# Windowed attention into a gated mixture: mixture scores, tails and values as fp32 products in quarters of the array, in a new order

## The chip, the core and the metric

One core of one Trainium2 chip runs the whole program. The metric is the device time of one execution in microseconds (us), the median of several runs.

## What is computed

Windowed causal attention over 8 batches, 8 heads and 576 positions, and then a mixture of four small attention experts over its output, of which a gate keeps two for each position. Cut to what matters:

```python
scores = scale * np.matmul(q, k.transpose(0, 1, 3, 2))          # head_dim 64
scores = np.where(mask, scores + bias[None], -1000000000.0)     # 0 <= rel < 128
attn = softmax(scores)
x = (attn @ v).transpose(0, 2, 1, 3).reshape(B, S, H * D)       # 8 x 576 x 512
for e in range(4):                                              # experts, 64 wide
    q, k, v = x @ wq[e], x @ wk[e], x @ wv[e]
    a = softmax(np.where(causal, -1000000000.0, scale * (q @ k.transpose(0, 2, 1))))
    out += gate_weight[:, :, e] * (a @ v @ wo[e])               # two experts of four
```

## The kernel before

The 576 positions are four blocks of 128 (`NQ = 4`) and a tail of 64 (`TAIL`). The attention takes one pair of heads at a time, 32 pairs `g`, four to a batch `b`. The mixture takes one pair of experts at a time, `pr` = 0 and 1 for each batch, with row `j` = 0 or 1 of the pair in the lower or upper 64 partitions. So a (b, pr) unit occurs 16 times.

The tensor engine (PE) is used whole (128*128) or cut into tiles: 128*64 are two column halves, 64*128 two row halves, and 64*64 four quarters. Tiles that share no rows and columns work side by side. An fp32 product takes two passes, so it shows as two matmul rows of the trace; a float32r product or a transpose shows as one.

Attention works in quarters, in fp32 (`attn_s`, `attn_pv`), and its values already come from two PSUM tiles, one for each half of the keys, which are added on VectorE. The mixture works otherwise:

- `qkproj` writes q and k of an expert pair as a float32r cast (`QH`, `KH`) and a float32r remainder (`QL`, `KL`), each by one cast and one subtraction from PSUM.
- `moe_s` makes the scores of the four blocks as three float32r terms (two for block 0), 22 matmuls on row halves of 64*128 for each (b, pr), over the full causal width 128(i+1) of a block of 128 query rows.
- `moe_s_tail` makes the tail's scores for both rows j at once from a block-diagonal copy of the tail queries (`QJ`, rounded into place by `pool_round`), with six matmuls of 288 columns on the whole array for each (b, pr).
- `moe_t` transposes the probabilities (`turn` does so in pairs of 64*128 tiles; the last tail block is one 128*128 transpose).
- `moe_pv` multiplies them by the values, 8 fp32 matmuls on column halves (128*64) into one PSUM tile, then a cast to `AH` and a subtraction from PSUM to `AL`; `moe_pv_tail` does the same for the tail, 10 matmuls.
- `moe_wo` multiplies `AH` and `AL` by the split output weights `WOH` and `WOL`: for each block of 128 positions first the three terms of pr 0 (WOH·AH, WOL·AH, WOH·AL), then the three of pr 1.

At the start the program works on block 0 and 1 of the four head pairs of batch 0 (`half_s` with x = 0) as soon as their first loads are there, while PE repeats a filler matmul (`warm`).

What sets the order: all engine operations are recorded, and `plan` replays them by the numbers of a packed table `ORDER`, which also chooses the engine where an operation has two (`nc.any`) and says where filler matmuls stand. `place` issues them, so that nearly every instruction has line 1189 in the trace (1225 in the kernel after). Each engine and each DMA queue runs its own instructions in that order. The loads go through SyncE's queue (SP), four of the start through ScalarE's.

## Time and profile before

| | us |
|---|---|
| median of 3 runs | 472.25 |
| lowest and highest run | 471.92, 472.99 |
| the profiled execution | 473.2 |
| its span, first to last instruction | 471.4 |
| busy in it: PE, VectorE (DVE), ScalarE (ACT), GpSimd (POOL) | 462.7, 409.3, 370.5, 222.7 |

The profiled execution is 0.95 us above the median, and 1.8 us of it lie outside the span. A timeline row tells when a run of like matmuls starts and how long it lasts. Ends of matmuls are modelled: the next row starts before the end of the last one, so what a run costs is read from its start to the next row's start.

### The profile page before, as it was taken

The numbers are of one execution on the slowest core, as the hardware profiler recorded it, in microseconds if no ns is written. First come the engines' busy times: TensorE is split into PE (matmuls) and PEld (weight loads), VectorE is DVE, ScalarE is ACT, GpSimd is POOL, SyncE is SP. The second block draws the span as 40 slices with busy tenths as digits, with TensorE's granted clock in tenths as the row PEclk, the third lists the DMA queues.
The fourth block names the chain that finished last, engine by engine and source line by source line (L and its number), as shares of the span: only waits on it lengthen the run. The fifth ranks groups of instructions, "written<-read, shape, count | busy, mean of one in ns | idle before, by whom it ended". The sixth has DMA issues, their size and how long they took to land.

```text
span 471.4 us, 17542 instructions
## 1 busy us (share of the span) xinstructions
PE 462.7 (98%) x6380; PEld 403.8 (86%) x6380; DVE 409.3 (87%) x1894; ACT 370.5 (79%) x1409; POOL 222.7 (47%) x464
## 2 busy tenths in 40 slices
PE   7999999999999999999999999999999999999996
PEld 5788999897889789797898987898789897899775
DVE  6999999979998998879989798798999979966852
ACT  5968879989978688796989798897976959833952
POOL 4833968183916346261470907426263623561430
PEclk9999999999999999999999999999999999999999
DMA  7899410345320653150441281602731030300033
GB/s 202 266 221 246 112 52 1 77 103 141 108 80 0 139 142 117 29 140 1 115 129 37 80 189 39 180 2 61 205 121 38 3 86 2 120 1 1 3 113 112
DMA packets 29862, 44.99 MB, mean 95 GB/s; under 512 B 9424, under 2 KB 15824, under 8 KB 29776
## 3 DMA queue, kind: packets, MB, share of 16 engines
q1 hardware_dynamic: 29040, 43.42, 34.0%
q8 instruction: 50, 0.82, 0.8%
q10 hardware_dynamic: 736, 0.46, 0.4%
q14 instruction: 36, 0.29, 0.2%
HBM read 34.42 MB, written 9.44 MB: 93 GB/s over the span
## 4 chain that ended last, share of the span: by engine, by line
PE 84%; DMA 5%; SPq 3%; DVE 3%; ACT 2%; POOL 1%; issue 1%; DVEq 0%
PE ps L1189 84%; DMA w<-in_hd 4%; SPq L1189 3%; DVE w L1189 2%; ACT w L1189 2%; POOL w L1189 1%; DMA w<-in_wall 1%; DVE ps L1189 1%; DVE WL L1189 0%; DVE ALm L1189 0%; ACT AHm L1189 0%; DVE mr L1189 0%; DVE nm L1189 0%; POOL QJm L1189 0%; DVE ALTm L1189 0%
## 5 line engine op out<-in xcount | busy, mean ns | idle before, releaser
L1189 ACT COPY w<-ps 128x256 f32<-128x256 f32 (+2 forms) x232 | 92.4, 443 | 29.8 <-PE ps L1189 21.3
L1189 PE MATMUL ps<-wx,WH 128*128 128x288 f32 (+2 forms) x512 | 110.4, 300 | 0.0
L1189 ACT ACTIVATE w<-w,nm 128x128 f32<-128x128 f32 x252 | 98.9, 397 | 7.3 <-DVE nm L1189 5.8
L1189 POOL TENSOR_SCALAR w<-w,mr,w 128x256 f32<-128x256 f32 (+3 forms) x128 | 78.2, 622 | 43.2 <-DVE mr L1189 24.1
L1189 POOL TENSOR_SCALAR w<-w,r 128x128 f32<-128x128 f32 x177 | 64.6, 378 | 68.3 <-PE ps L1189 25.4
L1189 PEld LDWEIGHTS ps<-wx,WH 128*128 128x128 f32 x512 | 83.2, 190 | 1.5 <-issue 0.3
L1189 ACT ACTIVATE w<-w,mnm 128x512 f32<-128x512 f32 (+3 forms) x128 | 71.2, 558 | 10.0 <-DVE mnm L1189 9.4
L1189 DVE TENSOR_TENSOR w<-ps,tmt 128x768 f32<-128x768 f32 (+3 forms) x96 | 72.5, 770 | 3.3 <-PE ps L1189 2.2
L1189 DVE CUSTOM_DVE_ANT_0 w<-ps,tbt 128x128 f32<-128x128 f32 x288 | 71.7, 283 | 1.1
L1189 PE MATMUL ps<-wx,WL 128*128 128x288 f32 (+2 forms) x256 | 71.9, 298 | 0.0
L1189 PE MATMUL ps<-WH,wx 128*128 128x260 f32 x288 | 61.5, 285 | 0.0
L1189 PE MATMUL ps<-w 64*64 64x192 f32 (+3 forms) x1256 | 58.6, 304 | 2.3 <-DMA w<-in_hd 1.7
L1189 PE MATMUL ps<-idt,w 64*128 64x64 f32 (+1 forms) x1152 | 58.6, 230 | 1.0 <-POOL w L1189 0.9
L1189 PEld LDWEIGHTS ps<-idt,w 64*128 64x128 f32 (+1 forms) x1152 | 47.4, 139 | 11.0 <-issue 3.4
L1189 PE MATMUL ps<-w,vt 64*64 64x192 f32 (+3 forms) x1344 | 56.3, 283 | 0.0
L1189 PEld LDWEIGHTS ps<-w,vt 64*64 64x64 f32 (+1 forms) x1344 | 50.0, 133 | 5.7 <-DVE r L1189 0.6
L1189 DVE COPY_PREDICATED ps<-mkt,ps 128x128 f32<-128x128 int32 (+2 forms) x160 | 49.2, 329 | 5.4 <-PE ps L1189 5.0
L1189 PEld LDWEIGHTS ps<-w 64*64 64x64 f32 (+1 forms) x1256 | 44.0, 134 | 8.6 <-DMA w<-in_hd 2.7
L1189 DVE CUSTOM_DVE_ANT_0 w<-ps,mtt 128x256 f32<-128x256 f32 (+2 forms) x96 | 49.8, 551 | 0.8 <-PE ps L1189 0.4
L1189 PEld LDWEIGHTS ps<-WH,wx 128*128 128x128 f32 x288 | 48.0, 189 | 0.8 <-issue 0.3
L1189 ACT ACTIVATION_READ_ACCUMULATOR w<-w,nm 128x1 f32 x252 | 48.6, 193 | 0.0
L1189 PE MATMUL ps<-w,w 128*64 128x64 f32 (+4 forms) x576 | 48.0, 319 | 0.0
(111 smaller groups left out, 947.5 us busy)
## 6 DMA issues: line engine op xcount, KB each, us to landing
w<-in_hd SPq DMA_DIRECT2D x56, 288.0 KB, 4.6
vt<-in_vd SPq DMA_DIRECT2D x28, 320.0 KB, 3.7
out<-w SPq DMA_DIRECT2D x31, 256.0 KB, 2.5
w<-in_hd SPq DMA_DIRECT2D x14, 128.0 KB, 3.5
w<-in_hd SPq DMA_DIRECT2D x56, 32.0 KB, 3.7
w<-in_wall SPq DMA_DIRECT2D x4, 386.0 KB, 6.6
out<-w SPq DMA_DIRECT2D x8, 128.0 KB, 3.3
vt<-in_vd SPq DMA_DIRECT2D x4, 192.0 KB, 3.8
```

The lines of the kernel that those rows point to most:

```text
L1189: getattr(getattr(tc.nc, e), m)(*a, **k)
```

## The change

Mixture scores, tails and values become fp32 products in 64*64 quarters. `qkproj` writes q and k once, unsplit, into `KK`; `QH`, `QL`, `KL` and `QJ` are gone. `moe_s` gives each half of 64 query rows its own causal width; in odd blocks the two row halves are swapped, with a second bias table `mts` for them. `moe_s_tail` treats both pairs of a batch at once, and `moe_t` transposes all five tail blocks in `turn`. `moe_pv` splits the keys between the row halves, into two PSUM tiles, which are then drained, added, rounded and subtracted.

```diff
-        hi, lo = (QH, QL) if isq else (KH, KL)
-        act_copy(hi[:, pr, sl], o, n)
-        dve_sub(lo[:, pr, sl], o, hi[:, pr, sl].bitcast(F32), n)
-        if isq and half == 1:
-            for x, q in ((0, QH), (1, QL)):
-                for j in range(2):
-                    d = slice(D * j, D * j + D)
-                    pool_round(QJ[d, pr, x, d], q[d, pr, S - TAIL :].bitcast(F32))
+        evac(KK[:, 0 if isq else 1, pr, sl], o)
...
         for i in blocks:
             n = P * (i + 1)
-            m = n if i else 2 * P
-            for x, (q, k) in enumerate(terms if i else terms[:2]):
-                for j in range(2):
-                    d = slice(D * j, D * j + D)
-                    k2 = k[d, pr, :n] if i else KK[d, :, pr, :P]
+            for j in range(2):
+                d = slice(D * j, D * j + D)
+                for y in range(2):
+                    m = P * i + D * (y ^ i & 1)
                     nc.tensor.matmul(
-                        ss[j][:, o : o + m], q[d, pr, P * i : P * (i + 1)], k2, start=(x == 0), stop=(x == (2 if i else 1))
+                        ss[j][D * y : D * y + D, o : o + m + D], KK[d, 0, pr, m : m + D], KK[d, 1, pr, : m + D], start=True, stop=True
                     )
...
-                softmax_block(ss[j][:, o : o + n], pt, mtt[:, 512 - n : 512] if i else pt, nm[:, c : c + 1], n)
+                softmax_block(ss[j][:, o : o + n], pt, (mts if i % 2 else mtt)[:, 512 - n : 512], nm[:, c : c + 1], n)
```

```diff
-    def moe_s_tail(b, pr):
+    def moe_s_tail(b):
         st = m2s[b]
-        nm, sm = st[pr, "nm"], st[pr, "sm"]
-        pt = MPL[pr]
         ss = []
+        stats(b, 1)
         for half in range(2):
-            s = ps_s.tile([P, 512], F32, tag="s", name=f"msl{b}_{pr}_{half}")
-            ss.append(s)
+            ss.append([ps_s.tile([P, 512], F32, tag="s", name=f"msl{b}_{half}_{j}") for j in range(2)])
             sl = slice(HALF * half, HALF * (half + 1))
-            for k, (x, w) in enumerate(((0, KH), (1, KH), (0, KL))):
-                nc.tensor.matmul(s[:, :HALF], QJ[:, pr, x, :], w[:, pr, sl], start=(k == 0), stop=(k == 2))
...
+            for j in range(2):
+                d = slice(D * j, D * j + D)
+                for pr in range(2):
+                    nc.tensor.matmul(
+                        ss[half][j][D * pr : D * pr + D, :HALF], KK[d, 0, pr, NQ * P :], KK[d, 1, pr, sl], start=True, stop=True
+                    )
...
+                softmax_block(ss[half][j][:, :HALF], MPL[j][:, sl], bias, dst, HALF, init=init)
+        for j in range(2):
```

```diff
-        parts = ([(0, 0), (1, 0)], [(0, 1), (0, 3), (1, 1), (1, 3)], [(0, 2), (1, 2)], [("tail", c) for c in range(NQ)])[u]
-        n = 8 if u < 2 else 4
-        pc = (tw if u < 2 else big2).tile([P, n * P], F32, tag="pt", name=f"mpt{b}_{pr}_{u}")
+        parts = ([(0, 0), (1, 0)], [(0, 3), (0, 1), (1, 1), (1, 3)], [(0, 2), (1, 2)], [("tail", c) for c in range(NQ + 1)])[u]
+        n = (8, 8, 4, 5)[u]
+        pc = (big2 if u == 2 else tw).tile([P, n * P], F32, tag="pt", name=f"mpt{b}_{pr}_{u}")
...
-            evac(pc.rearrange("p (a n) -> p a n", n=P)[:, :, D * h : D * h + D], ts[h][:, :n, :], n * D)
-        if u == 3:
-            t = ps_t.tile([P, P], F32, tag="t", name=f"mt{b}_{pr}_4")
-            nc.tensor.transpose(t, st["p"][pr, "tail"][:, NQ * P :], idt)
-            pc = st["pt"][pr, "tail", NQ] = tr.tile([P, P], F32, tag="pt", name=f"mpt{b}_{pr}_4")
-            evac(pc, t, P)
-
-    def moe_pv(b, pr, c):
+            if u == 3:
+                evac(v[:, :, D * h : D * h + D], ts[h][:, :n, :])
+            elif u == 1:
+                o = D - D * h
+                evac(spread(pc, o, (3 * P, 3), (P, 2)), spread(ts[h].rearrange("p a n -> p (a n)"), 0, (3 * D, 3), (D, 2)))
+                evac(v[:, 2:6:3, D - o : 2 * D - o], ts[h][:, 2:6:3, :])
+            else:
+                evac(spread(pc, D * h, (2 * P, n // 2), (3 * D - P * h, 2)), ts[h][:, :n, :].rearrange("p (a b) n -> p a b n", b=2))
```

```diff
+    def moe_pv(b, pr):
         st = m2s[b]
+        xa, ya = (ps_a.tile([P, 512], F32, tag="m", name=f"{n}{b}_{pr}") for n in ("ma", "mb"))
...
-        n = 512 - P * c
-        for j in range(2):
-            e = 2 * pr + j
-            nc.tensor.matmul(
-                acc[D * j : D * j + D, P * c :], V2[:, c, D * e : D * e + D], st["pt"][pr, j, c][:, :n],
-                start=(c == 0), stop=True, skip_group_check=True,
-            )
-        if c == NQ - 1:
-            act_copy(AH[:, pr, :512], acc, 512)
-            dve_sub(AL[:, pr, :512], acc, AH[:, pr, :512].bitcast(F32), 512)
-
-    def moe_pv_tail(b, pr):
+        for c in range(NQ):
+            for y, dst in enumerate((xa, ya)):
+                r, f = slice(D * y, D * y + D), D * y
+                for j in range(2):
+                    e = 2 * pr + j
+                    nc.tensor.matmul(
+                        dst[D * j : D * j + D, P * c + f :], V2[r, c, D * e : D * e + D], st["pt"][pr, j, c][r, f : 512 - P * c],
+                        start=(c == 0), stop=True, skip_group_check=True,
+                    )
+        tmp = big2.tile([P, DM], F32, tag="xs", name=f"ma{b}_{pr}t")
+        evac(tmp, xa)
+        nc.vector.tensor_tensor(tmp[:, D:], tmp[:, D:], ya[:, D:], add)
+        rnd(AH[:, pr, :512], tmp)
+        ssub(AL[:, pr, :512], tmp, AH[:, pr, :512].bitcast(F32))
```

```diff
+        ta, tb_ = (ps_t.tile([P, 512], F32, tag="t", name=f"mal{b}_{y}") for y in range(2))
         for c in range(NQ + 1):
-            for j in range(2):
-                e = 2 * pr + j
-                src = pt[pr, "tail", c][:, D * j : D * j + D]
-                nc.tensor.matmul(
-                    acc[D * j : D * j + D, :TAIL], V2[:, c, D * e : D * e + D], src,
-                    start=(c == 0), stop=(c == NQ),
-                )
+            for y, dst in ((0, ta), (1, tb_))[c // NQ :]:
+                r = slice(D * y, D * y + D)
+                for pr in range(2):
+                    for j in range(2):
+                        e = 2 * pr + j
+                        nc.tensor.matmul(
+                            dst[D * j : D * j + D, D * pr : D * pr + D], V2[r, c, D * e : D * e + D], pt[j, "tail", c][r, D * pr : D * pr + D],
+                            start=(c + pr == 0), stop=True, skip_group_check=True,
+                        )
         o = TAIL * (b % 2)
-        ht, lt = AHT[:, pr, o : o + TAIL], ALT[:, pr, o : o + TAIL]
-        act_copy(ht, acc[:, :TAIL], TAIL)
-        dve_sub(lt, acc[:, :TAIL], ht.bitcast(F32), TAIL)
+        ht, lt = AHT[:, :, o : o + TAIL], ALT[:, :, o : o + TAIL]
+        tt = p2.tile([P, P], F32, tag="xq2", name=f"xm{b}", bufs=1)
+        evac(tt, ta[:, :P])
+        nc.vector.tensor_tensor(tt, tt, tb_[:, :P], add)
+        v = tt.rearrange("p (a n) -> p a n", n=TAIL)
+        rnd(ht, v)
+        ssub(lt, v, ht.bitcast(F32))
```

In the attention the four tail-score matmuls of a head pair all read the upper 64 partitions, where the tail keys get a tile `ku` of their own. Before, two read the lower (64 columns each) and two the upper (128 columns each); now the upper ones make all 64 and 128 columns.

```diff
+        nc.sync.dma_start(ku[D:], a[D:, QW + NQ * P : QW + S])
         nc.sync.dma_start(r[D:, 2 * S + TAIL :], a[D:, QW + (NQ - 1) * P : QW + NQ * P])
         nc.sync.dma_start(r[D:, 2 * S : 2 * S + TAIL], a[D:, NQ * P : S])
-        prepped[g] = (None, None, None, vt, r)
+        prepped[g] = (None, None, ku, vt, r)
 
...
-            lo, up = e[:D], e[D:]
+            up, s = e[D:], ss[1]
             x, m = 2 * S, S + (NQ - 1) * P
-            c, w = slice(3 * P, 3 * P + TAIL), slice(3 * P, 4 * P)
-            nc.tensor.matmul(ss[0][:D, c], lo[:, NQ * P : S], lo[:, m + P :][:, :TAIL], start=True, stop=True)
-            nc.tensor.matmul(ss[0][D:, c], lo[:, x : x + TAIL], lo[:, x + TAIL : x + 2 * TAIL], start=True, stop=True)
-            nc.tensor.matmul(ss[1][:D, w], up[:, x : x + TAIL], up[:, x + TAIL :], start=True, stop=True)
-            nc.tensor.matmul(ss[1][D:, w], up[:, :TAIL], up[:, m : m + P], start=True, stop=True)
-            nc.vector.copy_predicated(ss[1][:, c], mkt[:, P:], ss[0][:, c])
+            q0, q1, k0, k1 = up[:, x : x + TAIL], up[:, :TAIL], up[:, x + TAIL :], up[:, m : m + 3 * D]
+            nc.tensor.matmul(s[:D, 2 * P + D : 3 * P], q0, ku[D:], start=True, stop=True)
+            nc.tensor.matmul(s[D:, P : P + D], q1, k1[:, P:], start=True, stop=True)
+            nc.tensor.matmul(s[:D, 3 * P :], q0, k0, start=True, stop=True)
+            nc.tensor.matmul(s[D:, 3 * P :], q1, k1[:, :P], start=True, stop=True)
+            nc.vector.copy_predicated(s[:D, 3 * P : 3 * P + TAIL], mkt[:D, P:], s[:D, 2 * P + D : 3 * P])
+            nc.vector.copy_predicated(s[D:, 3 * P : 3 * P + TAIL], mkt[D:, P:], s[D:, P : P + D])
```

At the start the first blocks are computed causally, block 1 over all its 256 keys, with a bias table `FT` (kept in `KK`) that holds the mask, and without the predicated copies. The transposes of these blocks go from 16 to 24. The DMAs of `tmt` and `mkt` move from ScalarE's queue to SP's, the zeroing of PSUM goes, and `ORDER` is a new table.

```diff
-        part = products(ss, 2 * x, [q, q], k, tbt[:, p], 2, 5 * x)
+        if x == 0:
+            first_blocks(g, ss, q, k, FT[:, NP_ - 1 - g])
+            return
...
+    def first_blocks(g, ss, q, k, tb):
+        nm, sm, pt = state[g, 0]
+        for i in range(2):
+            n = P + P * i
+            for h in range(2):
+                d = slice(D * h, D * h + D)
+                for y in range(2):
+                    m = P * i + D * y
+                    nc.tensor.matmul(
+                        ss[h][D * y : D * y + D, P * i : P * i + n], q[h][d, m : m + D], k[d, :n], start=True, stop=True
+                    )
...
+                v = pt[:, 3 * h + i : 3 * h + 2 * i + 1, :]
+                bias = tb[:, h, 1 - i :, :].bitcast(F32)
+                softmax_block(a, v, bias, nm[:, c : c + 1], P + P * i)
+                exp_block(None, v, nm[:, c : c + 1], sm[:, c, 0:1], P + P * i)
...
-    fetch(0, 1, 0)
+    for g in range(4):
+        fetch(g, 1, 0)
     nc.scalar.dma_start(idt, ident)
-    nc.scalar.dma_start(tmt, tm)
-    nc.scalar.dma_start(mkt[:, P:], mk[:, P:])
-    nc.vector.tensor_scalar(mkt[:, :P], tbt[:, 3, 0, :], -1.0e6, None, op0=ALU.is_lt)
+    nc.vector.tensor_scalar(FT[:, 3, :, 0, :], tbt[:, 3, 0:3:2], -1.0e6, NEG, op0=ALU.is_ge, op1=mul)
+    nc.vector.tensor_tensor(FT[:, 3, :, 0, :], FT[:, 3, :, 0, :].bitcast(F32), tbt[:, 3, 1:4:2], add)
+    nc.gpsimd.tensor_scalar(FT[:, 3, :, 1, :], tbt[:, 3, 0:3:2], 1.0, 0.0, op0=mul, op1=add)
...
-    for t in ps_s.real:
-        tc.nc.vector.memset(t[D:, : 3 * P].rearrange("p (a n) -> p a n", n=P)[:, :, :D], 0.0)
```

Weights are split in two column pieces (`wprep`), and there are more buffers for probabilities: pools of 8, 4, 3 and 6 slots (`pp`, `tw`, `tr`, `big2`) become 9, 6, none and 5.

SP's queue at the start of the program, before. `w_90` and `w_91` get the heads of the first blocks (`in_hd`), `w_83` and `w_86` the weights, `vt` the values:

```order
L1189 DMA w_90<-in_hd 64x2x256 x4
L1189 DMA w_91<-in_hd 64x2x256 x4
L1189 DMA w_90<-in_hd 128x2x128
L1189 DMA w_90<-in_rd 128x2x320
L1189 DMA w_90<-in_hd 64x2x256 x2
L1189 DMA w_83<-in_wall 128x772
L1189 DMA vt_128<-in_vd 128x256
```

And after, where `w_91` and `w_92` are these two:

```order
L1225 DMA ku_148<-in_hd 64x64
L1225 DMA ku_151<-in_hd 64x64
L1225 DMA ku_156<-in_hd 64x64
L1225 DMA mts<-in_mt 64x512 x2
L1225 DMA w_91<-in_hd 64x2x256 x4
L1225 DMA w_92<-in_hd 64x2x256 x4
L1225 DMA w_91<-in_rd 128x2x320
L1225 DMA w_91<-in_hd 64x2x256 x2
L1225 DMA vt_125<-in_vd 128x256
L1225 DMA vt_126<-in_vd 128x256
L1225 DMA w_83<-in_wall 128x772
```

Five DMAs that the program needs later now stand ahead of the first heads' loads, and the values stand ahead of the first weights.

PE in the middle of the program, batch 2, from the values of pr 1 on. Before (`KKm,QHm` and `KKm,QLm` are scores, `WOH,AHm` is the output product that needs these values):

```order
L1189 MATMUL ps_74<-w_95,w_86 64x512 x2
L1189 MATMUL ps_74<-w_96,w_86 64x384 x2
L1189 MATMUL ps_74<-w_102,w_86 64x256 x2
L1189 MATMUL ps_74<-w_96,w_86 64x128 x2
L1189 MATMUL ps_72<-KKm,QHm 128x512
L1189 MATMUL ps_69<-KKm,QHm 128x512
L1189 MATMUL ps_72<-KKm,QLm 128x512
L1189 MATMUL ps_69<-KKm,QLm 128x512
```

And after:

```order
L1225 MATMUL ps_70<-KKm 64x512
L1225 MATMUL ps_70<-KKm 64x448
L1225 MATMUL ps_74<-w_95,w_87 64x512 x2
L1225 MATMUL ps_72<-w_95,w_87 64x448 x2
L1225 MATMUL ps_74<-w_99,w_87 64x384 x2
L1225 MATMUL ps_72<-w_99,w_87 64x320 x2
L1225 MATMUL ps_69<-KKm 64x64
L1225 MATMUL ps_69<-KKm 64x128
L1225 MATMUL ps_76<-KKm 64x64
L1225 MATMUL ps_76<-KKm 64x128
```

Scores and values now share the quarters and stand between one another, where there was a change of tile shape between them; the values fill two PSUM tiles. Between the last values matmul and the first output product stand 30 matmuls in the order before (the 22 scores, a transpose and 7 projections of 288 columns), and 39 in the order after (26 transposes of 64*128 tiles, one on the whole array and 12 projections).

## Rows read from the trace of the kernel before

**Rows 1.** The page: busy time by engine, and the chain that ended last.

```profile
PE 462.7 (98%) x6380; PEld 403.8 (86%) x6380; DVE 409.3 (87%) x1894; ACT 370.5 (79%) x1409; POOL 222.7 (47%) x464
PE 84%; DMA 5%; SPq 3%; DVE 3%; ACT 2%; POOL 1%; issue 1%; DVEq 0%
```

**Rows 2.** Busy time by window: from:to, length, busy us of each engine (x instructions).

```profile
200.00:300.00 100.00, 99.33 (x1406) 88.62 (x1399) 86.63 (x411) 85.69 (x331) 49.71 (x105) 1.00 0.36 95
300.00:400.00 100.00, 99.37 (x1405) 86.55 (x1405) 91.75 (x423) 81.26 (x315) 39.84 (x88) 1.00 0.26 74
```

**Rows 3.** PE's timeline in batch 2: start, length, operation (modelled end).

```profile
213.41 2.18 PE L1189 MATMUL ps<-idt,w 64*128 64x64 f32 x64
215.53 2.37 PE L1189 MATMUL ps<-w,w 128*64 128x512 f32 x16
217.83 0.50 PE L1189 MATMUL ps<-KKm,QHm 64*128 64x512 f32 x2
...
219.85 0.33 PE L1189 MATMUL ps<-idt,w 128*128 128x128 f32 x1
...
220.41 0.43 PE L1189 MATMUL ps<-wx,WH 128*128 128x288 f32 x2
220.68 0.29 PE L1189 MATMUL ps<-wx,WL 128*128 128x288 f32 x1
...
220.94 0.39 PE L1189 MATMUL ps<-WOH,AHm 128*128 128x512 f32 x1
```

**Rows 4.** PE's timeline: one set of attention scores in quarters, and the row behind.

```profile
50.93 1.42 PE L1189 MATMUL ps<-w 64*64 64x192 f32 x32
52.29 0.39 PE L1189 MATMUL ps<-WH,wx 128*128 128x260 f32 x1
```

**Rows 5.** PE's timeline: tail scores of the mixture between output products.

```profile
397.11 0.40 PE L1189 MATMUL ps<-WOH,ALm 128*128 128x512 f32 x1
397.34 0.57 PE L1189 MATMUL ps<-KKm,QJm 128*128 128x288 f32 x3
397.75 0.40 PE L1189 MATMUL ps<-WOH,AHm 128*128 128x512 f32 x1
```

**Rows 6.** PE's timeline: tail values of the mixture.

```profile
464.44 0.57 PE L1189 MATMUL ps<-w,w 128*64 128x64 f32 x12
464.94 0.39 PE L1189 MATMUL ps<-WOH,AHm 128*128 128x256 f32 x1
```

**Rows 7.** PE's timeline where attention scores end and attention values begin.

```profile
224.85 0.32 PE L1189 MATMUL ps<-w,vt 64*64 64x192 f32 x1
224.86 0.27 PE L1189 MATMUL ps<-w 64*64 64x128 f32 x1
```

**Rows 8.** SP's queue at the start: when DMAs are issued, and how long that takes.

```profile
0.73 5.97 SPq L1189 DMA_DIRECT2D w<-in_hd  x9
...
9.18 0.90 SPq L1189 DMA_DIRECT2D vt<-in_vd  x2
```

**Rows 9.** PE's timeline at the start: the first scores, and later ones.

```profile
4.81 3.69 PE L1189 MATMUL ps<-w 64*64 64x128 f32 x52
...
12.77 1.53 PE L1189 MATMUL ps<-w 64*64 64x192 f32 x32
```

**Rows 10.** Groups by shape: operation xcount | busy us, mean ns | idle before, releasers.

```profile
L1189 ACT COPY w<-ps 128x512 f32<-128x512 f32 x99 | 56.1, 590 | 16.2 <-PE ps L1189 15.4
...
L1189 POOL TENSOR_TENSOR wx<-w,wx 128x512 fp32r<-128x512 f32 x17 | 22.2, 1309 | 0.5
...
L1189 DVE TENSOR_TENSOR w<-w,ps 128x448 f32<-128x448 f32 x28 | 17.1, 612 | 1.2 <-ACT w L1189 0.6 <-PE ps L1189 0.2 <-issue 0.2
...
L1189 DVE TENSOR_TENSOR KKm<-ps,KKm 128x288 fp32r<-128x288 f32 x28 | 12.5, 450 | 2.6 <-ACT KKm L1189 2.3
...
L1189 POOL TENSOR_SCALAR wx<-w 128x512 fp32r<-128x512 f32 x19 | 11.8, 624 | 27.5 <-DVE w L1189 23.1 <-ACT w L1189 3.7 <-DVE ps L1189 0.3
...
L1189 DVE TENSOR_TENSOR ALm<-ps,AHm 128x512 fp32r<-128x512 f32 x16 | 11.0, 686 | 1.1 <-ACT AHm L1189 0.8
```

More of the change, by code (lines that the diff above doesn't have):

```diff
@@ L312, in attn_moe_kernel @@
     prepped = {}
+    half = {}
     SM = [cp.tile([P, 9, 2], F32, name=f"sm{k}") for k in range(2)]
@@ L663, in attn_moe_kernel, with terms @@
     AA = {}
+    def terms(late):
+        return sorted(((c, j) for c in range(4) for j in range(3)), key=lambda z: late and z[1] == 2)
     def vproj(b, t):
@@ new lines, in moe_s_tail @@
+            for j in range(2):
+                nm = st[j, "nm"]
+                bias = mtt[:, 0:HALF] if half == 0 else mtt[:, 512:]
+                init = BIG if half == 0 else nm[:, 9:10]
+                dst = nm[:, 9:10] if half == 0 else nm[:, 8:9]
+                softmax_block(ss[half][j][:, :HALF], MPL[j][:, sl], bias, dst, HALF, init=init)
+        for j in range(2):
+            nm, sm = st[j, "nm"], st[j, "sm"]
+            for half in range(2):
+                sl = slice(HALF * half, HALF * (half + 1))
+                exp_block(ss[half][j][:, :HALF], MPL[j][:, sl], nm[:, 8:9], sm[:, 16 + half : 17 + half], HALF)
+            st["p"][j, "tail"] = MPL[j]
@@ L943, in wload @@
             nc.sync.dma_start(mtt, mt)
+            for y in range(2):
+                nc.sync.dma_start(mts[D * y : D * y + D], mt[D - D * y : 2 * D - D * y, : NQ * P])
         wst[c] = w
@@ L1000, in f @@
             if tail:
-                moe_pv_tail(b, pr)
+                moe_pv_tail(b)
             else:
-                for c in range(NQ):
-                    moe_pv(b, pr, c)
+                moe_pv(b, pr)
             live[0] -= 0 if tail else 7
```

370 lines of the change are left out of this document (181 added, 189 removed).

## The prediction

> **What bounds the kernel now.** I read the page first: PE is busy for 462.7 of 471.4 us, VectorE for 409.3, and PE makes 84% of the chain that ended last [rows 1]. Then the windows: in the body PE works for 99.3 of each 100 us, while VectorE has 8 to 13 us to spare, ScalarE 14 to 19 and POOL half [rows 2]. So the body is worth what PE has to do, and an edit on another engine counts only if it delays PE or uses up that slack. Last the timelines, from the start of one run to the start of the next. Two places do not follow this rule: the start, where PE waits for loads and for the first softmax [rows 8, 9], and the end.
>
> **Prices on PE.** A run inside one tile shape loses less than one that ends with a change of shape: the modelled end lies 0.17 us behind the next start where the shape stays (397.11 + 0.40 against 397.34) [rows 5], but only 0.06 to 0.07 us where it changes (52.35 against 52.29; 217.90 against 217.83) [rows 3, 4]. A change costs 0.10 us. The set of attention scores takes 52.29 - 50.93 = 1.36 us; less one change, 1.26 us for 32 rows, four side by side, is 8 passes of 192 columns, 0.82 ns for a column and pass [rows 4]. The values give 0.86: 16 rows, two side by side, 2560 column passes in 2.30 - 0.10 = 2.20 us [rows 3]. I use 0.84.
>
> **Scores, 16 units.** Before, 217.83 to 219.85 is 2.02 us, or 1.92 without its change [rows 3]. After, each row half runs the widths 64, 128, ... 512, 2304 columns, over two quarters side by side, 1152 columns in each; two passes: 2304 x 0.84 ns = 1.94 us. Three cheap terms become one dear one at half the width: +0.02 x 16 = +0.3 us.
>
> **Tail scores.** Three matmuls of 288 take 0.41 us, 0.137 each [rows 5]; 12 to a batch are 1.64 us. After, four quarters of 2 x 288 columns and two passes: 0.97 us. -0.67 x 8 = -5.4 us. This is the largest term, since before half of the block-diagonal operand was zeros.
>
> **Values.** The column halves already fill the array, so quarters bring no more throughput: the lower row half has 1280 columns, 2.15 us against 2.20. The upper half has 1024, 1.72 us. If the halves keep step, the unit costs what the longer one does: 0 to -0.8 us in all, taken as 0.
>
> **Attention tails.** 64 columns more on the upper quarters, two passes, 0.108 us, 28 times (the first four pairs are made otherwise): +3.0 us if the halves keep step; the lower half gets 64 columns less, -3.0 us, if they do not.
>
> **Tail values.** Before, 12 rows take 0.50 us, less a change 0.40, 0.033 each [rows 6]; 40 rows to a batch are 1.33 us. After, 10 matmuls of 64 columns in the upper quarters, two passes: 1.08 us (8 in the lower: 0.86). -0.25 x 8 = -2.0 us.
>
> **Transposes and changes of shape.** 32 tail transposes more in 64*128 tiles at 2.12 / 64 = 0.033 us [rows 3] are +1.1 us; the 16 on the whole array that go gave back about as much, at 0.09 us each (219.85 is one, before the projections), -1.4 us. I set both to 0. Along PE the tile shape changes 153 times in the order before and 125 times after; 28 x 0.10 = -2.8 us.
>
> In step, PE's sum is 0.3 - 5.4 + 0 + 3.0 - 2.0 + 0 - 2.8 = **-6.9 us**.
>
> Do the halves keep step? Where scores end and values begin, a values matmul starts at 224.85, ahead of a scores matmul at 224.86 [rows 7]: a half runs ahead, but by one pass, not a unit. The Trainium skill has both answers: "TensorEngine Tiling (Array Packing)", section Key Properties, says that tiles operate independently; "TensorE: Matmul & The Clock Gate", Part 3, section The mechanism, says that matmuls start and end strictly in program order. By the second the sum is the -6.9 us; by the first it is that of the rival below. The row leans to the second.
>
> **The other engines.** VectorE and ScalarE lose the split of q and k: subtractions of 450 ns [rows 10], for keys and for queries, 64 in all, against 16 additions of 612 ns and some copies. POOL takes most of the new subtractions at 1309 ns; it is idle half the time [rows 2]. None becomes the bound. What is late next is the chain behind the values. Before: a cast and a subtraction of 0.69 us. After: drain 0.59, add 0.61, round 0.62, subtract 1.31 on POOL, 3.13 us [rows 10]. The cover in batch 2: before, 217.83 to 220.94, 3.1 us [rows 3]; after, 26 transposes (0.86), one more (0.09), 12 projections at 0.135 (1.62) and two or three changes, 2.8 us, and then the three products of pr 0 at 0.23 [rows 5], 0.7 us. The rounded part is wanted after 3.5 us and is there after 1.8, the remainder is wanted after 4.0 and there after 3.1. It holds, with some 0.9 us left for hand-overs and queueing; in the last batch less stands between. Bounds: 0, and 8 x 0.5 = 4; taken: **+0.8 us**.
>
> **The start.** SP needs 5.97 us for nine DMAs, 0.66 each, and 0.45 for a `vt` [rows 8]. Five DMAs now stand ahead of the first heads' loads: 5 x 0.45 to 5 x 0.66 = 2.3 to 3.3 us. Nothing hides that: the first scores start at 4.81 when their load has landed, and PE runs without long gaps only from 12.77 on [rows 9], so what the first loads lose goes through to the end. The weights and `vt` come later by as much. In return VectorE drops eight predicated copies there, but ScalarE has exponentials twice as wide and PE eight more transposes; I let these cancel. Bounds: 0 (the wait only replaces another one, as the masks come from ScalarE's queue) and 3.3; taken: **+2.8 us**. The eight PSUM memsets that go lay ahead of the first load's landing and are worth 0.
>
> **Sum.** 473.2 - 6.9 + 0.8 + 2.8 = 469.9 us for an execution like the profiled one, which stood 0.95 us above the median; against the median, **469.0 us**.
>
> **The rivals.**
> - The row halves run on their own, each through a whole run of quarters. Then the lower one sets the end: values -0.8, attention tails -3.0, tail values -0.47 x 8 = -3.8, with scores, tail scores and changes -15.5; the upper gives -7.7 + 3.0 - 2.0 and so -14.6. The slower counts, -14.6 in place of -6.9: 461.3 us; half way, 465. For it: scores and values now alternate in one shape. Against: the lead of one pass [rows 7].
> - Slower: the chain behind the values is late. Its four steps cross ScalarE, VectorE and POOL, of which the first two are busy for some 81 to 92% [rows 2], so each can queue for half a microsecond behind something else, and the 0.9 us are gone twice over. With 1 us of PE waiting behind the values of pr 1 in each of the eight batches: 469.0 + 8 = 477 us. It decides from 0.4 us a batch, where the gain of 3.25 is used up. For it: the cover shrinks from 3.1 us, of which 1.3 were needed, to one of 4.0, of which 3.1 are. Against: in the body PE waits for under 1 us in 100 now.
> - No gain: the changes of shape bring nothing, since the work between them drains anyway (+2.8), and the start costs 3.3 (+0.5): 472.3 us.
>
> **How the numbers follow.** Chances: the forecast 0.48, halves on their own (wholly or half) 0.14, slower 0.23, no gain 0.15. From this kernel's runs, 0.2% (0.95 us) is about what a measurement can tell from no change, so faster is below 471.3 and slower above 473.2. The forecast's own spread (start 0 to 3.3, cover 0 to 4) puts a tenth of it above 471.3. Faster: 0.43 + 0.14 + 0.02 = 0.59; same 0.05 + 0.11 = 0.16; slower 0.25. The range runs from half way to the free halves to nearly all of the slow case: 464.5 to 476.5 us.
>
> **What would show it.** The first scores at about 7.6 us and the same lateness at the first long run of PE; tail scores of a batch near 1.0 us; values units still near 2.2 us, not 1.7; about 125 changes; no PE wait for `AHm` or `ALm` behind the values. Wrong: PE waits named after ScalarE, VectorE or POOL in the body (the slow rival), or quarters whose halves drift apart by a microsecond.

## The result, and the profile after

The changed kernel takes **477.0 us** (476.07 to 477.15, four runs) against 472.4 us beside it on the same chip: 1.0092 times as long, 95% interval 1.0075 to 1.0110. The forecast was 469.0, so it is 8 us too low and on the wrong side. The clock is not the reason: the one execution of the changed kernel with a mean granted clock of 0.999 took 477.1 us, the three at 0.995 and 0.996 took 476.1 to 477.2.

The page of the changed kernel, busy time by engine and the chain that ended last, to be held against [rows 1], and two windows of its body, against [rows 2] (from:to, length, then busy us of PE, PE's weight loads, VectorE, ScalarE, POOL; granted clock; DMA share; GB/s):

```profile
PE 464.1 (98%) x7100; PEld 404.2 (85%) x7100; DVE 400.8 (84%) x1863; ACT 364.8 (77%) x1375; POOL 240.9 (51%) x449
PE 20%; POOL 2%; DVE 1%; ACT 0%; issue 0%; POOLq 0%
```

```profile
200.00:300.00 100.00, 99.59 (x1586) 88.97 (x1579) 89.22 (x427) 82.44 (x315) 47.75 (x92) 1.00 0.33 86
300.00:400.00 100.00, 99.36 (x1668) 87.73 (x1668) 87.11 (x419) 79.53 (x300) 49.38 (x95) 1.00 0.27 75
```

PE is still busy for over 99 of 100 us, and VectorE does less than before (400.8 us against 409.3): by its busy times, the page shows no reason for a loss. The chain of the changed kernel is traced back only some 110 us from the end, where its shares sum to 23%, so its 20% of PE is not to be held against the 84% of [rows 1].

The waits of PE in the whole span, first the changed kernel, then the one before (us in all, times, the longest; only waits that leave PE visibly idle are in this list):

```profile
PE ps L1225 <- DMA w<-in_hd: 2.4, 3, 1.9
PE ps L1225 <- POOL w L1225: 2.1, 5, 1.1
PE ps L1225 <- POOL AHTm L1225: 1.1, 1, 1.1
PE ps L1225 <- DVE lg L1225: 0.5, 1, 0.5
...
```

```profile
PE ps L1189 <- DMA w<-in_hd: 1.7, 3, 0.7
PE ps L1189 <- DVE ps L1187: 1.3, 1, 1.3
PE ps L1189 <- POOL w L1189: 0.9, 2, 0.5
PE ps L1189 <- DVE w L1189: 0.4, 1, 0.4
```

These lists explain little: 4.6 us are lost, and with the two small lines left out they differ by 2.3. The experiments below show that most of the waiting lies inside what counts as busy.

**The start.** SP's queue and PE's timeline in the changed kernel, against [rows 8] and [rows 9] (start, length, operation; in brackets the idle time ahead and what ended it):

```profile
0.73 1.87 SPq L1225 DMA_DIRECT2D ku<-in_hd  x3
2.65 1.24 SPq L1225 DMA_DIRECT2D mts<-in_mt  x2
3.93 5.20 SPq L1225 DMA_DIRECT2D w<-in_hd  x8
```

```profile
6.75 0.44 PE L1225 MATMUL ps<-w 64*64 64x128 f32 x4 [1.87 <-DMA w<-in_hd]
7.42 5.31 PE L1225 MATMUL ps<-w 64*64 64x128 f32 x60 [0.24 <-DMA w<-in_hd]
...
45.53 0.71 PE L1225 MATMUL ps<-idt,w 64*128 64x64 f32 x16
```

The five added DMAs take 3.1 us of issue, and the first scores start at 6.75 us in place of 4.81. The last row is the mark for the end of the start in all that follows: the first transposes of the main attention. In the kernel before they stand at

```profile
43.24 0.72 PE L1189 MATMUL ps<-idt,w 64*128 64x64 f32 x16
```

so the start lost 2.3 us. From this mark to PE's last matmul, the **body**, it is 424.1 us before and 426.3 after: the other half of the loss, in the part that was to win 6.

### The profile page after: what moved, and what is told of

It is laid out like the page before. It is cut to its first block, busy times and chain, and to the rows that moved or that the text cites. A ratio compares the mean times of both kernels' runs of the same rounds, so it can differ in the third digit from the quotient of the medians.

```text
span 475.4 us, 18911 instructions
## 1 busy us (share of the span) xinstructions
PE 464.1 (98%) x7100; PEld 404.2 (85%) x7100; DVE 400.8 (84%) x1863; ACT 364.8 (77%) x1375; POOL 240.9 (51%) x449
## 5 line engine op out<-in xcount | busy, mean ns | idle before, releaser
L1225 ACT COPY w<-ps 128x512 f32<-128x512 f32 (+4 forms) x231 | 94.2, 452 | 43.7 <-PE ps L1225 33.4
L1225 POOL TENSOR_SCALAR w<-w,mr,w 128x512 f32<-128x512 f32 (+3 forms) x128 | 77.8, 617 | 47.7 <-DVE mr L1225 22.6
L1225 POOL TENSOR_SCALAR w<-w,r 128x128 f32<-128x128 f32 (+1 forms) x166 | 61.8, 385 | 52.7 <-DVE r L1225 23.8
L1225 ACT ACTIVATE w<-w,mnm 128x384 f32<-128x384 f32 (+3 forms) x128 | 71.2, 558 | 6.4 <-DVE mnm L1225 6.4
L1225 DVE TENSOR_TENSOR w<-ps,tmt 128x768 f32<-128x768 f32 (+2 forms) x92 | 69.3, 776 | 4.8 <-PE ps L1225 4.6
L1225 PE MATMUL ps<-w 64*64 64x128 f32 (+3 forms) x1200 | 65.8, 314 | 2.4 <-DMA w<-in_hd 2.4
L1225 DVE COPY w<-ps 128x128 f32<-128x128 f32 (+5 forms) x115 | 49.5, 451 | 12.9 <-PE ps L1225 11.2
L1225 DVE COPY_PREDICATED ps<-mkt,ps 128x256 f32<-128x256 int32 (+3 forms) x180 | 53.4, 316 | 3.2 <-PE ps L1225 1.0
L1225 PE MATMUL ps<-w,w 64*64 64x64 f32 (+7 forms) x1088 | 53.0, 307 | 0.0
L1225 PE MATMUL ps<-KKm 64*64 64x288 f32 (+8 forms) x640 | 51.1, 411 | 0.0
```

Of the source, the lines that this page charges most:

```text
L1225: getattr(getattr(tc.nc, e), m)(*a, **k)
```

## The experiments

In all of them the time is a median, and the kernel before ran beside each on the same chip (472.1 to 472.4 us).

### Is the start lost in SP's queue?

`e1_five_dmas_later` issues the five DMAs behind the first weights; `e2_before_five_dmas` gives the kernel before five DMAs of the same sizes.

```diff
+    sp = [i for i, o in enumerate(seq_) if o[0] == "sync"]
+    five, to = sp[:5], sp[27]
+    seq_ = [o for i, o in enumerate(seq_[: to + 1]) if i not in five] + [seq_[i] for i in five] + seq_[to + 1 :]
```

> The kernel after, with its five early DMAs (three ku, two mts) moved in SP's queue from the front to behind the first weights and masks; nothing else is changed. Theory: the start of the kernel after loses about 3 us to these five DMAs (3.2 us of issue time in its trace, first scores at 6.75 us instead of 4.81). Then the first scores start at about 4 us and the time falls from 477.0 to 474.0 to 475.0. Rival: the start is set by the new first blocks (wider exponentials, more transposes), so the time stays within 0.7 us of 477.0 although the loads come earlier.

> The kernel before, with five DMAs of the same sizes (64x64 three times, 1 KB rows on 64 partitions twice) put ahead of its first loads; what they write is overwritten before it is read. Theory: the delay of the first loads goes through to the end undiminished, 472.4 + 2.5 to 3.2 = 475 to 475.6 us. Rival: waits behind it absorb most, under 473.5 us.

Measured: e1 477.0 us (ratio to before 1.0114, 1.0072 to 1.0157), nothing won. That is the number of the rival, which blames the new first blocks; the trace shows another reason. e2 476.1 us (1.0088, 1.0067 to 1.0110): 3.9 us for five small DMAs in a kernel that is otherwise the old one, a little more than the theory's range, and the mark moves from 43.24 to 47.47 us. In e1 the first scores do start at 4.81 us again, but the gain is given back later (SP's queue, then PE's timeline):

```profile
15.98 1.78 SPq L1228 DMA_DIRECT2D ku<-in_hd  x3
17.81 1.66 SPq L1228 DMA_DIRECT2D mts<-in_mt  x2
```

```profile
24.59 3.02 PE L1228 MATMUL ps<-w 128*128 128x192 f32 x34 [1.99 <-DMA w<-in_rd]
```

In the first 20 us SP's queue has only short pauses, up to 1 us, so the five push back whatever stands behind them, wherever they stand. What helps is another queue. `e8_five_dmas_on_scalar`:

```diff
+    sp = [i for i, o in enumerate(seq_) if o[0] == "sync"]
+    five = sp[:5]
+    ai = [i for i, o in enumerate(seq_) if o[0] == "scalar" and o[1] == "dma_start"][1]
+    seq_ = [o for i, o in enumerate(seq_[: ai + 1]) if i not in five] + [("scalar", *seq_[i][1:]) for i in five] + [o for i, o in enumerate(seq_) if i > ai and i not in five]
```

> The changed kernel, complete, with the five new input DMAs at the start issued by ScalarE in place of SyncE. Theory: SP's queue is full for its first 20 us, and 3.2 us of issues there push every later block back; without them the time falls by 2.3 to 3.5 us, to 473.5 to 474.8 us, and TensorE's first scores start near 4.8 us. Rival: the clock or the bandwidth sets the start, and it makes no difference which queue issues: 476.3 to 477.5 us.

Measured: 475.4 us (1.0064, 1.0049 to 1.0079), 1.6 us less than the changed kernel, and the mark at 44.04: 1.5 of the 2.3 us of the start are back, so the five DMAs and not the first blocks made most of that loss; the time gained is less than expected. PE's timeline of e8, its first scores and its mark:

```profile
4.81 0.77 PE L1229 MATMUL ps<-w 64*64 64x128 f32 x8
...
44.04 0.71 PE L1229 MATMUL ps<-idt,w 64*128 64x64 f32 x16
```

### Did PE's own work fall, and who eats the gain?

`e3_light_after` and `e4_light_before` leave out the scaling of the probabilities (310 instructions of GpSimd and 122 of ScalarE in the changed kernel) and VectorE's predicated copies, e3 in the changed kernel and e4 in the one before. With less to wait for, their bodies come near to what PE needs by itself. (e4, and e14 below, have eight filler matmuls of 512 columns in place of many of 256.)

```diff
     def scl(dst, src, r, early=False):
+        nc.alt["drop"].add(len(nc.ops))
...
+        nc.alt["drop"].add(len(nc.ops))
         nc.vector.copy_predicated(ss[1][:, c], mkt[:, P:], ss[0][:, c])
```

> The kernel after without the scaling of the probabilities (most of it on POOL, some on ScalarE) and without the predicated copies on VectorE; this work is left out, PE's program is the same. Theory: in the body PE lost some 8 us waiting for POOL's scaling and for VectorE to empty PSUM, 6 us more than before; without that work these waits go, and 477.0 falls to 469.5 to 471.5, 1 to 2 us below the kernel before with the same left out. Rival: PE's own work in quarters got slower, the waits are only its shadow: 475 us or more, and still 3 to 5 us above the kernel before with the same left out.

> The kernel before without the same scaling and predicated copies, and with 8 filler matmuls of 512 columns at the start in place of 16 of 256. Its trace shows 2 us of waits in the body, 1.5 of them for loads, so both theories expect little: 470.5 to 472 us. It is the measure for the kernel after without the same work.

Measured: e3 466.1 us (0.9871, 0.9855 to 0.9887), below its theory's range, e4 470.7 us (0.9973, 0.9955 to 0.9991). The bodies are 415.2 and 422.3 us: **PE's own work fell by some 7 us**: 7.1 by these two, and 7.9 if the 1.3 and 0.5 us in which PE stands idle in the two bodies are taken off. An estimate from four runs of each PE program (changed kernel, e1, e3, e6; before, e2, e4, e14) agrees: the fastest of the four for each stretch of 30 matmuls, added up from the mark to the start of the last matmul, gives 412.4 us after and 420.0 before. By the same count e3 has 414.9 and e4 422.0, the two full kernels 426.0 and 423.8. Against the light runs the full kernels' bodies hold 11.1 us more (426.3 - 415.2) after the change and 1.8 (424.1 - 422.3) before it. The gain was there, and 9 us more than before went to waiting for other engines.

`e5_no_scaling` and `e6_no_predicated_copies` leave out one of the two in the changed kernel, `e14_before_no_predicated_copies` the copies in the kernel before.

> The changed kernel without the scaling of the probabilities by the reciprocal of their sum (GpSimd's multiplications ahead of the transposes, with the few of them that ScalarE does), so that GpSimd is lightly used; the predicated copies on VectorE stay. With both left out the changed kernel took 466.1 us. Theory A, TensorE waits mostly because GpSimd is late with the scaled probabilities: 468 to 470.5 us. Theory B, it waits mostly because VectorE empties PSUM late: 474 us or more. Both in parts: 471 to 473 us.

> The changed kernel without VectorE's predicated copies, the scaling on GpSimd stays. Theory A (GpSimd late with the scaled probabilities): 474 us or more. Theory B (VectorE empties PSUM late): 468 to 470.5 us. Both in parts: 471 to 473.5 us.

> The kernel before without VectorE's predicated copies (some 50 us of its work), and with eight filler matmuls of 512 columns in place of its many of 256; the scaling stays. Both left out gave 470.7 us against 472.2. If VectorE bounds the kernel before as it does the changed one (where the same gave 7.9 us): 464 to 467 us. If TensorE and VectorE stand level there, so that relief of either alone brings little: 470 to 471.5 us.

Measured: e5 473.5 us (1.0021, 1.0004 to 1.0038); e6 469.1 us (0.9938, 0.9923 to 0.9953); e14 472.4 us (0.9991, 0.9976 to 1.0006). In the changed kernel the scaling is worth 3.5 us and the copies 7.9, together 10.9 (e3): VectorE for the larger part, GpSimd and ScalarE, which share the scaling, for the rest. So theory A falls; B holds in e6, while e5 lies just under its range. In the kernel before the same copies are worth nothing, which is less than either theory of e14 allowed. The pages of e6 and e14:

```profile
PE 457.1 (98%) x7100; PEld 401.9 (86%) x7100; DVE 358.1 (77%) x1683; ACT 362.6 (78%) x1375; POOL 241.8 (52%) x449
```

```profile
PE 461.8 (98%) x6372; PEld 402.1 (85%) x6372; DVE 374.4 (79%) x1734; ACT 369.3 (78%) x1409; POOL 223.3 (47%) x464
```

Both are rid of 35 to 43 us of VectorE's work; only the changed kernel was waiting for it. In e6, PE's busy time falls by 7 us (464.1 to 457.1) with every matmul still there: so much waiting had been counted as busy.

### Is the body worth what PE has to do?

That was the prediction's rule. `e11_less_pe_after` and `e12_less_pe_before` leave out the products of AH with the low part of the output weights, 16.4 us of PE, in the changed kernel and in the one before; the other engines keep all their work.

```diff
             for lhs, rhs in ((hi, WOH), (hi, WOL), (lo, WOH)):
+                if rhs is WOL:
+                    nc.alt["drop"].add(len(nc.ops))
                 nc.tensor.matmul(acc, lhs[:, pr, sl], rhs[:, pr, :], start=(k == 0), stop=(k == 5))
```

> The changed kernel without the products of AH with the low part of the output weights (68 matmuls of 512 columns and 8 of 256, at 0.23 us between two starts 16.4 us of TensorE, spread over all batches); every instruction of the other engines stays, so the output lacks this correction. If the body is worth what TensorE has to do (the prediction's rule): 477.0 - 16.4 = 460.6 us, between 459 and 463. Theory F, the body is held by VectorE emptying PSUM, and a faster TensorE only waits more: under half of the cut arrives, 469 to 474 us.

> The kernel before with the same matmuls left out. By the prediction's rule 472.2 - 16.4 = 455.8 us, between 454 and 458. Theory F as a limit that already stood beside the kernel before, 2 to 5 us below its time: 462 to 470 us; if the limit came only with the change (its order, its two PSUM tiles), the kernel before still gains nearly all, 454 to 459 us.

Measured: e11 475.2 us (1.0068, 1.0048 to 1.0088), e12 468.9 us (0.9941, 0.9920 to 0.9961). Of 16.4 us, 1.8 arrive after the change and 3.2 before it; e12 lies in theory F's range, e11 still above it. This is the clearest result of all: **both kernels stand on a limit that is not this work of PE**, the kernel before some 3 us above it, the changed one some 2. In e11's profiled execution the granted clock was half for 3.4 us of the body (from 404.8 us), which can have eaten at most 1.7 us of the cut; e12's body ran at 1.00. Page and waits of e12, then of e11:

```profile
PE 452.7 (97%) x6304; PEld 391.5 (84%) x6304; DVE 408.5 (88%) x1894; ACT 369.7 (79%) x1409; POOL 222.0 (48%) x464
```

```profile
PE ps L1195 <- POOL w L1195: 3.0, 5, 1.1
PE ps L1195 <- DVE w L1195: 2.4, 4, 1.5
...
```

```profile
PE 454.3 (96%) x7024; PEld 390.9 (83%) x7024; DVE 400.6 (85%) x1863; ACT 364.1 (77%) x1375; POOL 241.3 (51%) x449
```

```profile
PE ps L1231 <- POOL w L1231: 2.9, 4, 2.0
PE ps L1231 <- DVE w L1231: 2.4, 4, 0.8
...
```

PE still reads 96 and 97% busy, with 16 us of it gone. Waits named after POOL and VectorE have come in its place, and the rest does not show as idle time.

### Which part of the change raised the limit?

`e9_old_attention_tails` makes the attention's tail scores as before (two row halves, one copy of 128 partitions, no `ku`); `e10_old_tails_mts_on_scalar` also moves the two `mts` DMAs to ScalarE's queue.

```diff
-            nc.tensor.matmul(s[:D, 2 * P + D : 3 * P], q0, ku[D:], start=True, stop=True)
...
+            nc.tensor.matmul(ss[0][:D, c], lo[:, NQ * P : S], lo[:, m + P :][:, :TAIL], start=True, stop=True)
...
-            nc.vector.copy_predicated(s[D:, 3 * P : 3 * P + TAIL], mkt[D:, P:], s[D:, P : P + D])
+            nc.vector.copy_predicated(ss[1][:, c], mkt[:, P:], ss[0][:, c])
```

> The changed kernel, complete, with the attention's tail scores and their one predicated copy as before the change; the three DMAs of ku at the start go with that, the two of mts stay ahead. What this undoes is 64 columns more on the upper quarters for each of 28 head pairs (3.0 us of TensorE if the row halves keep step) and one more predicated copy for each of them on VectorE (28 x 0.23 = 6.4 us more instructions there, 5.5 by the rows of the copies), and three of the five DMAs at the start (up to 1 of the 1.6 us that moving all five gave). Theory C, TensorE pays for the columns and VectorE's extra copies delay it only by their share (all copies, 54 us of VectorE, were worth 8 us of the time): 477.0 - 3.0 - 0.9 - 1.0 = 472 us, between 471 and 473. Theory D, the extra copies stand in each pair's path and cost their whole length: 467 to 470 us. Rival E, the row halves do not keep step, the columns cost nothing, VectorE has slack for the copies: 475 to 477 us.

> As the one before, and the two mts DMAs issued by ScalarE: SP's queue begins as in the kernel before. If SP's queue is what the start lost, another 0.6 to 1.5 us less than e9_old_attention_tails; under theory C 470 to 472 us, under D 466 to 469, under E 474 to 476.

Measured: e9 473.7 us (1.0039, 1.0015 to 1.0062), e10 472.4 us (1.0009, 0.9991 to 1.0028). Theory C comes nearest; both lie above its range. The two undo several things at once (the second copy, the columns, the `ku` loads, the start), and which of them counts how much these runs do not part. The second copy is plain in VectorE's rows by line and form (count, then busy us and mean ns), before and after:

```profile
L1189 DVE COPY_PREDICATED ps<-mkt,ps 128x64 f32<-128x64 int32 x32 | 7.1, 222 | 1.2 <-PE ps L1189 1.1
```

```profile
L1225 DVE COPY_PREDICATED ps<-mkt,ps 64x64 f32<-64x64 int32 x56 | 12.6, 229 | 1.2
```

At 64 columns a copy over 64 partitions takes as long as one over 128, so splitting it doubled it. `e13_less_pe_old_tails` takes the 16.4 us of PE out of e10, with the edit of e11.

> e10_old_tails_mts_on_scalar (472.4 us) without the products of AH with the low part of the output weights, as in e11_less_pe_after; it asks where the other engines' limit lies once the start and the attention's tails are as before the change. If these two parts make the whole difference between the limits (475.2 us with the change, 468.9 before): 468.5 to 469.5 us. If the new order and the two-tile values keep a part of it: 470 to 472 us. If TensorE set the end in e10: 456 to 460 us.

Measured: 469.9 us (0.9949, 0.9926 to 0.9972), between the first two ranges. The limit falls from 475.2 to 469.9, to within 1 us of that of the kernel before (468.9): these two parts, the start's DMAs and the attention's tails, make 5.3 of the 6.3 us by which the change raised it (each of the three times is known to about 1 us).

### Two that did not come out as hoped

`e7_rounding_off_gpsimd` gives the rounding behind the values to ScalarE and the subtraction to VectorE.

```diff
-        rnd(AH[:, pr, :512], tmp)
-        ssub(AL[:, pr, :512], tmp, AH[:, pr, :512].bitcast(F32))
+        nc.any(*[("scalar", "copy", (AH[:, pr, :512], tmp), None)] * 2)
+        o = ("vector", "tensor_tensor", (AL[:, pr, :512], tmp, AH[:, pr, :512].bitcast(F32), sub), None)
```

> The changed kernel, complete, with the rounding behind the values of the mixture moved from GpSimd to ScalarE and the subtraction behind it from GpSimd to VectorE, two of VectorE's operations later than it stood: GpSimd is relieved, VectorE gets more. Theory A (GpSimd late): 472.5 to 475.5 us. Theory B (VectorE late): 477.5 to 481 us. If neither engine's load counts, but only the order of the work: 476.3 to 477.5 us.

Measured: 497.0 us (1.0516, 1.0487 to 1.0545), 20 us more than the changed kernel and far outside every theory. VectorE's load rose by 8 us, to that of the kernel before (409.0 us busy); but the moved instructions stand in the queues of engines that everything else passes through. The largest waits of PE in e7 and one of VectorE:

```profile
PE ps L1233 <- DVE lg L1233: 5.4, 2, 4.9
PE ps L1233 <- ACT AHm L1233: 4.3, 2, 2.2
...
```

```profile
...
DVE ALm L1233 <- ACT AHm L1233: 7.4, 4, 4.3
...
```

The rounding waits on ScalarE for VectorE's addition, the subtraction on VectorE for the rounding, and what stands behind both waits too. The granted clock also fell to half three times in the body, for 3.4 us each (from 222, 301 and 362 us), which is at most 5 of the 20 us. On GpSimd, half idle, the same steps did not cost this. The run says little on which engine is late, and was not a fair test of it.

`e15_start_shared` starts from e10 and spreads the start further, to see whether a version beats both kernels.

```diff
+    two, three, to = sp[:2], [sp[10], sp[13], sp[14]], sp[38]
...
+        + [("scalar", *seq_[i][1:]) for i in three]
...
+        + [seq_[i] for i in two]
```

> e10_old_tails_mts_on_scalar, complete, with the first load of in_rd and the first two of vt on ScalarE's queue, and the two of mts on SP's after its full first 25 us. If SP's queue sets the start there too (TensorE waits 2.3 us for loads in the first 24 us of e10): 1 to 2 us less, 470.4 to 471.4 us, a little below the kernel before. If the first softmaxes set it: 472 to 473 us.

Measured: 471.9 us (0.9987, 0.9968 to 1.0007). PE waits only 0.2 us for a load in the first 24 us, and yet the mark stays at 43.31 us (43.42 in e10). The two marks are not alike, though: in this execution of e15 the granted clock was half from 8.3 to 11.7 us, in that of e10 it was not. Of the executions with a mean clock of 0.999 or more, the two of e15 took 471.7 us and the six of e10 the same (median), so the loads taken off SP's queue brought nothing. No version measurably beats the kernel before.

## Why the prediction was wrong

**The sum on PE was right, partly by luck.** -6.9 us were predicted, 7 to 8 found, but some terms were off and made up for one another. The tail scores went from 13.46 to 8.44 us (start to next start, summed over their 96 and 128 rows), -5.0 where -5.4 was said. Two values units and the tail values of the last batch, on PE's timeline, against [rows 3] and [rows 6]:

```profile
457.31 4.53 PE L1225 MATMUL ps<-w,w 64*64 64x512 f32 x64
461.77 0.53 PE L1225 MATMUL ps<-idt,MPL 64*128 64x64 f32 x10
...
463.82 1.66 PE L1225 MATMUL ps<-w,w 64*64 64x64 f32 x72
465.41 0.50 PE L1225 MATMUL ps<-WOH,ALm 128*128 128x512 f32 x1
...
466.60 0.96 PE L1225 MATMUL ps<-WOH,ALm 128*128 128x512 f32 x3 [0.22 <-POOL ALm L1225]
```

(461.77 - 457.31 - 0.10) / 2 = 2.18 us for a values unit, as said. The tail values were mis-sized: 1.49 us after the change's 0.10, not 1.08. In the trace the single rows of a quarter follow at 58 ns a pass (0.91 ns a column), which makes 1.17 us for 20 passes, -1.3 in place of -2.0 for the eight batches; the other 0.3 us here pass before the row at 464.15, from which on they follow at this rate. Nor was the price of 0.82 ns read rightly from [rows 4]: eight of the 32 rows there are 128 columns wide, as a view that keeps the shapes apart shows, so that a quarter has 1408 and not 1536 column passes and the price is 0.89.

```profile
L1189 PE MATMUL ps<-w 64*64 64x192 f32 x24 | 1.4, 331 | 0.0
L1189 PE MATMUL ps<-w 64*64 64x128 f32 x8 | 0.4, 269 | 0.0
```

The 0.84 that was used holds for the values all the same: 2.18 us for 2560 column passes are 0.85.

**The row halves do not keep step.** PE in the changed kernel where values (`w,w`) and attention scores with their tails (`w`) stand between one another:

```profile
88.04 1.02 PE L1225 MATMUL ps<-w,w 64*64 64x512 f32 x8
88.81 0.58 PE L1225 MATMUL ps<-w 64*64 64x192 f32 x8
89.13 0.91 PE L1225 MATMUL ps<-w,w 64*64 64x320 f32 x8
89.67 0.53 PE L1225 MATMUL ps<-w 64*64 64x192 f32 x6
```

From start to start these are 0.77, 0.32 and 0.54 us. At 0.84 ns for a column and pass the upper half's products, 448, 192 and 320 columns in two passes, take 0.75, 0.32 and 0.54; the lower half's, 512, 192 and 384, take 0.86, 0.32 and 0.65. So the upper half goes on as soon as it is free itself. The third row even starts with the upper half's 320 columns, while in the program the lower half's 384 stand first (y = 0 before y = 1 in `moe_pv`). The rule of the Trainium skill that matmuls start and end in program order ("TensorE: Matmul & The Clock Gate", Part 3, section The mechanism) does not hold here, though the prediction leaned to it. The lead comes to 0.2 us at the tails in this run of quarters, and there the 64 columns more can vanish behind the upper half's shorter values. Summed from start to next start, the 1040 rows of the attention's scores in the body take 38.8 us before (e4), 38.6 with the new tails (e3) and 38.4 with the old ones in the new order (e10). This is a rough measure, since products that stand between one another share the time, but it shows nothing of the +3.0. The times of e9 and e10 cannot show this term, since in the changed kernel PE's work hardly arrives (e11). The rival's -14.6 did not come either. With -5.0 for the tail scores, about 0 for the attention's tails and -1.3 for the tail values, the prediction's sum would have been -8.8 us, a little more than was found.

**The start was right in size**: 2.3 us against 2.8, inside 0 to 3.3. It was late by the issue time of five DMAs, but the first scores came at 6.75 and not at 7.6, the delay is a matter of the whole queue and not of what stands first (e1), and only 1.5 us of it went with the five DMAs (e8).

**The step that failed is the first one, on which all the rest stands: "the body is worth what PE has to do".** It was read from PE's 99.3 busy us in 100 [rows 2], with the slack of the others taken from their idle shares. e12 refutes it for the kernel before: 3.2 of 16.4 us arrive. So by that run no more than some 3 of the -6.9 us could have arrived, even with nothing else changed. What the runs show in its place is that each kernel has two limits: PE's own work with its start, and a limit of the other engines, which stays when PE has less to do (e11, e12). In the changed kernel the time falls when VectorE's copies or the scaling are left out (e6, e5).

| us | before | changed |
|---|---|---|
| measured | 472.4 | 477.0 |
| without scaling and copies (near PE's own limit) | 470.7 | 466.1 |
| 16.4 us of PE left out (near the others' limit) | 468.9 | 475.2 |

Before, PE's limit was the higher one by 2 us. The change lowered it by 4.6 us, the start's loss included, and raised the other by 6.3: the limits changed places, and that one is now 9 us above PE's. Each measured time stands some 2 us above the higher of its two.

The sign was in [rows 1]: PE's weight loads were busy for 86% and VectorE for 87% of the span. The Trainium skill says not to judge headroom by the busy share of matmuls, which are pipelined, but by that of the weight loads ("Perfetto Trace Analysis", section Identifying the Most-Contended Engine). By that measure VectorE and PE stood level before, which fits e12 and e14. It does not tell the cases apart by itself: in the light runs e3 and e4, near PE's own limit, the weight loads show 86% as well. "TensorEngine Tiling (Array Packing)", section PSUM Bottleneck, warns that tiles speed up TensorE but not the emptying of PSUM; e6 fits that, with 7.9 us for the copies that VectorE makes in PSUM ahead of the emptying.

**The term for the other engines, +0.8 us with bounds 0 to 4, was therefore some 9 us short** (11.1 - 1.8 by e3 and e4). It looked at one chain, the one behind the values, and that one held: PE waits for `ALm` once, 0.2 us, in the last batch (the row at 466.60). The slow rival named 477 us and was right on the number by accident: it placed the loss in this chain. And the part-by-part list left out an instruction that the diff shows, the second predicated copy of the attention's tails, 28 times 0.23 us on VectorE; what it alone costs was not run.

How the waiting looks where it does show, at the longest wait of the body: POOL's queue, and PE behind it.

```profile
55.47 1.04 POOL L1225 TENSOR_SCALAR WOH<-w 128x1024 fp32r<-128x1024 f32 x1 [2.74 <-DMA w<-in_wo]
...
56.48 0.72 POOL L1225 TENSOR_SCALAR w<-w,r 128x128 f32<-128x128 f32 x2
...
56.91 0.81 PE L1225 MATMUL ps<-idt,w 64*128 64x64 f32 x13 [1.09 <-POOL w L1225]
```

GpSimd waits 2.7 us for the load of the output weights; the scaling of a pair's probabilities stands behind that, and PE's transposes behind the scaling.

**What stays open.** Which chain makes the others' limit in the kernel before is not settled: without VectorE's copies alone it gains nothing, as PE then sets the end. That it runs through the eight PSUM tiles is argued, not shown. e11 to e13 leave out PE work of one kind only, the output products, and about the same part of it arrives in all three (1.8, 3.2 and 2.5 us of 16.4), however far apart the two limits are said to be; a chain that runs through others of PE's products would look the same. The new order by itself, against the old one on the same work, was not tried; e13 leaves it at most about 1 us of the limit's rise. That e10 stands 2.5 us above e13 fits two limits that add a little, and is not explained further.

## What to carry to other kernels

A busy share of 99% does not say that an engine's work is what the time is made of: leave out a known amount of its work and see how much of it arrives, before a saving there is priced in full. Where engines stand level, a saving on one is worth little more than the distance to the next limit, and what the same change adds elsewhere is paid in part (43 us of VectorE's copies were worth 7.9 us after the change, 35 us nothing before it). Do not read what a PE term costs from the time of a kernel that something else holds up. Count what is added to a queue that hardly pauses, such as the loads of a start, and to the engine that empties PSUM, instruction by instruction.

## What was not expected of the hardware

- Five DMAs of 16 and 64 KB whose data nothing reads cost 3.9 us of 472 when they stood ahead in SP's queue (e2; they take 3.15 us to issue). In the changed kernel, where `ku` is first read at 36 us and `mts` at 64, the five cost as much behind the first weights as in front of them (e1).
- The granted clock fell to half (1.2 in place of 2.4 GHz) in the changed kernel's start, after PE had waited 1.87 us for its first load and then worked in short pieces (windows, columns as above; the clock stands third from the end, and the last row is e15's). In e8, with the first scores at 4.81 us, it stayed at 1.00 in the same windows; but in e15, whose first scores also start at 4.81, it fell to half from 8.3 to 11.7 us, after PE had worked with pauses of 0.1 and 0.2 us only, so an early start alone does not keep it up.

```profile
5.00:7.00 2.00, 0.25 (x4) 0.20 (x4) 0.00 (x0) 0.00 (x0) 1.86 (x3) 1.00 0.57 153
...
9.00:10.50 1.50, 1.50 (x18) 0.96 (x22) 0.68 (x3) 1.02 (x4) 0.00 (x0) 0.50 0.67 192
10.50:12.00 1.50, 1.50 (x20) 0.98 (x18) 1.09 (x11) 1.33 (x6) 0.26 (x1) 0.50 0.89 288
...
9.00:10.50 1.50, 1.50 (x22) 1.26 (x22) 0.91 (x8) 1.48 (x7) 0.41 (x1) 0.50 1.05 245
```

- Executions of the kernel before with a mean granted clock of 0.998 or more took 472.1 us (median of 56), those at 0.995 and 0.996 473.5 us (10), in e10 471.7 and 473.5. Such short falls of the clock are part of the scatter.
- Row halves of the array drift apart by 0.1 to 0.2 us where one has less to do, and a product that stands later in the program then starts first.
- An fp32 matmul in a quarter costs 58 ns a pass at 64 columns, 0.91 ns a column, against 0.84 to 0.85 in the wide values.
- A predicated copy of 64x64 takes 229 ns, one of 128x64 222: half the partitions save nothing.
